# Two projections made in another order by strided matmuls, with contiguous copies, in a recurrence and long-convolution kernel

## The chip, the cores and the metric

The kernel runs on one core of a Trainium2 chip. The metric is the time of one execution on the device in microseconds (us), the median of three runs. Inside the core, five engines run side by side, each with its own queue of instructions in order: PE (TensorE, matrix products), DVE (VectorE), ACT (ScalarE), POOL (GpSimd) and SP (SyncE, which here issues the transfers). PEld stands for the weight loads of PE. On-chip memory is SBUF, and the banks that matmuls write are PSUM.

## What is computed

Two layers, one after the other, on 4 batches of 6272 time steps and 256 channels. First a gated recurrence, then a layer that multiplies two projections of its result with a circular convolution of a third.

```python
sig = 1.0 / (1.0 + np.exp(-f_logit))
f = lower_bound + (1.0 - lower_bound) * sig
for t in range(S):
    h = f[:, t] * h + (1.0 - f[:, t]) * x[:, t]
    y[:, t] = h
...
proj = y @ w_proj                        # 256 -> 3 * 256
x1, x2, x3 = the three thirds of proj
x2_conv = irfft(rfft(x2, axis=1) * rfft(filter_fft, axis=0), n=S, axis=1)
out = (x1 * x2_conv * x3) @ w_out
```

## The kernel before, in words

The state h is held for a whole batch in SBUF (tile HA) as fp16, channels on partitions and time along the free dimension, in two halves `kh` of 128 channels that start at columns HB[0] and HB[1]. The transform of length 6272 = 128 x 49 is split by the prime-factor method: time t is 49 m + r, with m from 0 to 127 and r from 0 to 48 (Q = 49). Between the two halves of h lies a region "A" of the same tile. It holds copies of h that continue a half past its end (the wraps), and later the spectrum.

The work of a batch b goes through these functions:

- `hgrn(b)`: 13 chunks of 512 steps. Two loads per chunk (f_logit and x, on SP), a sigmoid on ACT (L283), a product on POOL (L285), transposes on PE (L294), the gate's affine step from PSUM on ACT (L306) and the scan on DVE (L311), which writes h. After each scan a copy of h into region A (L320, the wraps), which the planner gives to DVE (it appears as L257) or POOL (L262).
- `phase_p(b)`: x2, by matmuls whose weights are columns of h taken at a stride of 49 (L590).
- `phase_f1(b)`: the first transform (L605), evicted by ACT or DVE into region A.
- `mini(b)`: a small transform of the frequencies at index 0 (L620). Its moving operand takes one fp16 of every 128.
- `units(b)`: 16 units. Each loads its part of the filter's spectrum (SP), transforms (L649, moving operand in runs of 64 fp16), multiplies on DVE (L659), copies zero frequencies on POOL (L652) and transforms back (L669); the result is evicted by ACT or DVE.
- `gate(b, u)`, called at the end of unit u: for the chunks in GATES[u], x1 and x3 for 10 values of m, so 490 steps (the last chunk 8, 392 steps), for two blocks `jb` of output channels. Two matmuls for each of x1 and x3 (L340) accumulate over `kh`; two ACT copies (L350) take them from PSUM to the tiles x1s and x3s; one product on POOL (L355) writes z. Each PSUM result is in the order (m, r) of time. The copies put it in the order (r, m) as they write, with steps of 40 bytes in SBUF (32 for the last chunk). There are 104 such matmuls and 52 such copies in a batch.
- `phase_o(b)`: the last transform (L695), the product with z on DVE (L702), the output projection (L712), evictions and the stores (SP).

The order on each engine comes from a planner (class Plan). Every piece of work is entered by `op` with the tokens that it reads and writes and its cost on each engine that may run it. `emit` then places piece after piece: among those whose inputs are placed it takes, for every engine, the one that can start first by these costs, and of equal ones the one with the longest path behind it. Where two engines are given, it chooses by the same costs. So a cost changes the order and the engine, and no instruction. `hgrn(b + 1)` overlaps units and `phase_o(b)`, and its first transposes of a chunk wait for a unit named in AFTER. A gate's matmuls wait for their chunks of h ("hn") and, by the token ("F", u), for the forward transform of their unit. The token "qT" is written by each group of transposes in turn, so that they keep their order.

Of the kernel before, what the change touches and what calls it, by code (L numbers as in the profile page):

```python
# [13 lines left out]
AOP = mybir.AluOpType  # L14
AF = mybir.ActivationFunctionType
# [9 lines left out]
Q = 49  # L25
# [3 lines left out]
NCHK = 13  # L29

AFTER = (2, 5, 7, 10, 12, 15)

GATES = [[u] if u < NCHK else [] for u in range(16)]
XR = 10
NEP = 128
UE = 8
# [2 lines left out]
ZS = 64.0  # L39
# [16 lines left out]
class Plan:  # L56
# [20 lines left out]
    def op(self, cost, fn, r=(), w=(), kb=0.0, table=None, take=0, src=None):  # L77
        preds = set()
        for t in r:
            if t in self.writer:  # L80
                preds.add(self.writer[t])
        for t in w:
            if t in self.writer:
                preds.add(self.writer[t])
            preds.update(self.readers.get(t, ()))
        me = len(self.ops)
        if src is not None:
            preds.add(src)
            self.ops[src]["users"].append(me)
        self.ops.append(dict(cost=cost, fn=fn, preds=preds, kb=kb, table=table, end=None,  # L90
                             eng=None, succ=[], take=take, src=src, users=[], at=None))
        for p in preds:
            self.ops[p]["succ"].append(me)
        for t in r:
            self.readers.setdefault(t, set()).add(me)
        for t in w:
            self.writer[t] = me
            self.readers[t] = set()
        return me
# [89 lines left out]
def kernel(  # L189
# [10 lines left out]
    nc = tc.nc  # L200
# [4 lines left out]
    op = plan.op  # L205
# [12 lines left out]
    W13 = konst.tile([128, 2, 512], F16, name="W13")  # L218
# [5 lines left out]
    HA = konst.tile([128, 2 * S + EW], F16, name="HA")  # L224
    A = HA[:, S:S + EW].rearrange("m (e r k) -> m e r k", r=2, k=64)
    HB = (0, S + EW)
# [5 lines left out]
    x1s = konst.tile([128, 2, CH], F32, name="x1s")  # L232
# [5 lines left out]
    PS = psp.tile([128, 8, 512], F32, name="PS")  # L238

    def E(a, z):  # L240

        return [("E", u) for u in range(a // 1024, (z - 1) // 1024 + 1)]
# [6 lines left out]
    def copy(e, dst, src, scale=None):  # L249
        if e == "ACT":  # L250
            if scale is None:
                nc.scalar.copy(dst, src)  # L252
            else:
                nc.scalar.activation(dst, src, AF.Copy, scale=scale)
        elif e == "DVE":
            if scale is None:
                nc.vector.tensor_copy(dst, src)  # L257
            else:
                nc.vector.tensor_scalar(dst, in0=src, scalar1=scale, scalar2=None,
                                        op0=AOP.mult)  # L260
        else:
            nc.gpsimd.tensor_copy(dst, src)  # L262

    def either(n, runs=1.0):

        return {"ACT": 0.06 + runs * n / 1200.0, "DVE": 0.08 + runs * n / 960.0}

    count = dict(x=0, f=0, s=0, o=0)

# [1 line left out]
    def hgrn(b):  # L271
        for c in range(NCHK):
            t0 = c * CH
            nb = min(CH, S - t0) // 128
            n = nb * 128
            k = count["x"] % NX
            count["x"] += 1
            xt, ft = XT[:, k, 0:nb], FL[:, k, 0:nb]
            for dst, src, t in ((ft, f_logit, ("ft", k)), (xt, x, ("xt", k))):
                op({"SP": 0.5}, lambda e, dst=dst, src=src, t0=t0, n=n: nc.sync.dma_start(  # L280
                    dst, src[b, t0:t0 + n, :].rearrange("(j p) d -> p j d", p=128)),
                   w=[t], kb=n)
            op({"ACT": 0.1 + 0.213 * nb}, lambda e, ft=ft: nc.scalar.activation(  # L283
                ft, ft, AF.Sigmoid, scale=-1.0), r=["sin"], w=[("ft", k)], table="sigmoid")
            op({"POOL": 0.1 + 0.535 * nb}, lambda e, xt=xt, ft=ft: nc.gpsimd.tensor_tensor(  # L285
                xt, xt, ft, op=AOP.mult), r=[("ft", k)], w=[("xt", k)])

            late = [("U", AFTER[min(c, len(AFTER) - 1)])] if b else []
            for kh in range(2):
                cols = slice(kh * 128, kh * 128 + 128)  # L290

                def turn(e, p, src, cols=cols, nb=nb):
                    for j in range(nb):
                        nc.tensor.transpose(PS[:, p, j * 128:(j + 1) * 128], src[:, j, cols],  # L294
                                            iden[:])
                sT = op({"PE": 0.108 * nb}, lambda e, p, f=turn, s=ft: f(e, p, s),
                        r=[("ft", k), "iden"] + late, w=["qT"], take=1)
                uT = op({"PE": 0.108 * nb}, lambda e, p, f=turn, s=xt: f(e, p, s),
                        r=[("xt", k), "iden"], w=["qT"], take=1)
                j = count["f"] % 2  # L300
                count["f"] += 1
                fT = fTs[:, j, 0:n]
                t1 = HB[kh] + t0
                h = HA[:, t1:t1 + n]
                op({"ACT": 0.13 + n / 1200.0}, lambda e, p, fT=fT, n=n, kh=kh:
                   nc.scalar.activation(fT, PS[:, p, 0:n], AF.Identity,  # L306
                                        scale=nomc[:, kh:kh + 1], bias=1.0),
                   r=["om"], w=[("fT", j)], src=sT)
                init = 0.0 if c == 0 else HA[:, t1 - 1:t1]
                op({"DVE": 0.07 + 2.25 * n / 1000.0}, lambda e, p, h=h, fT=fT, n=n, init=init:  # L310
                   nc.vector.tensor_tensor_scan(h, fT, PS[:, p, 0:n], init, op0=AOP.mult,  # L311
                                                op1=AOP.add),
                   r=[("fT", j)] + ([("hn", kh, c - 1)] if c else []), w=[("hn", kh, c)],
                   src=uT)

                a, o = (t0, t0) if kh == 0 else (max(t0, S - E1), EW - S + max(t0, S - E1))
                z = min(t0 + n, E0) if kh == 0 else t0 + n
                if z <= a:
                    continue
                op({"DVE": 0.08 + (z - a) / 3840.0, "POOL": 0.1 + (z - a) / 1000.0},  # L320
                   lambda e, a=a, o=o, z=z, kh=kh: copy(
                       e, HA[:, S + o:S + o + z - a], HA[:, HB[kh] + a:HB[kh] + z]),
                   r=[("hn", kh, c)], w=E(o, o + z - a))


    def gate(b, u):
        z = zt[b % 2]
        for c in GATES[u]:
            m0 = c * XR
            nm = min(XR, 128 - m0)  # L330
            hn = [("hn", kh, i) for kh in range(2) for i in range(max(c - 1, 0), c + 1)]
            t0, n = m0 * Q, nm * Q
            for jb in range(2):
                x13 = []
                for i in range(2):
                    js = slice(i * 256 + jb * 128, i * 256 + jb * 128 + 128)

                    def mm(e, p, js=js, t0=t0, n=n):
                        for kh in range(2):
                            nc.tensor.matmul(PS[:, p, 0:n], W13[:, kh, js],  # L340
                                             HA[:, HB[kh] + t0:HB[kh] + t0 + n],
                                             start=(kh == 0), stop=(kh == 1))
                    x13.append(op({"PE": 2 * n / 2400.0}, mm,
                                  r=hn + ["W13", ("F", u)], w=["qX"], take=1))
                j = count["s"] % 2
                count["s"] += 1
                xs = [t[:, j, 0:n] for t in (x1s, x3s)]
                for i in range(2):
                    op({"ACT": 0.16 + n / 1200.0}, lambda e, p, xs=xs[i], n=n, nm=nm, i=i:
                       nc.scalar.activation(  # L350
                           xs.rearrange("p (r m) -> p m r", m=nm),
                           PS[:, p, 0:n].rearrange("p (m r) -> p m r", r=Q), AF.Copy,
                           scale=1.0 if i else ZS), w=[("x1s", j, i)], src=x13[i])
                op({"POOL": 0.12 + 2.2 * n / 1000}, lambda e, xs=xs, nm=nm,
                   zz=z[:, jb, :, m0:m0 + nm]: nc.gpsimd.tensor_tensor(  # L355
                       zz, xs[0].rearrange("p (r m) -> p r m", m=nm),
                       xs[1].rearrange("p (r m) -> p r m", m=nm), op=AOP.mult),
                   r=[("x1s", j, 0), ("x1s", j, 1)], w=[("z", b % 2, jb, c)])


# [276 lines left out]
    def units(b):  # L637
        for u in range(NU):
# [26 lines left out]
            def inv(e, ib, k=k):  # L665
# [10 lines left out]
                PS[:, ib:ib + 2, 0:392].rearrange("p a (g c) -> p c a g", g=4)),  # L676
               r=[("x2", g) for g in range(13)], w=["Th", ("Th", u)], src=i2)
            gate(b, u)


# [112 lines left out]
```

## Time and profile before

| | us |
|---|---|
| three runs | 624.77, 627.38, 632.55 |
| median | 627.38 |
| the profiled execution | 630.62 |
| its span, first to last instruction | 628.7 |

| engine | busy us | share of the span |
|---|---|---|
| PE | 514.8 | 82% |
| ACT | 489.0 | 78% |
| DVE | 484.3 | 77% |
| PEld | 373.3 | 59% |
| POOL | 300.9 | 48% |

The profile is of one execution. A busy PE is not a PE at its peak: a matmul's row lasts until its result has passed through, and the next one starts meanwhile. The mean granted clock of PE was 0.939 of full speed. A row of a group gives its line, engine, operation, what is written from what, shape and count, then busy time and the mean length of one in ns, and behind the second bar the engine's idle time before such instructions. A row in order of time gives the start, the length from first start to last end, and the number of instructions merged. By the groups, the ACT copies of L350 are the longest part of ACT: 113.0 us for x1s and 113.9 us for x3s.

### The profile page before, as it was taken

Reading aid. Unit: us, or ns where it says so; the run is one execution under the profiler, and the core shown is the slowest. Engines: PE = TensorE matmul, PEld = TensorE weight load, DVE = VectorE, ACT = ScalarE, POOL = GpSimd, SP = SyncE. Lnnn points to the kernel's source line nnn. Section 1 sums busy time; section 2 is a strip of 40 time slices with the busy share of each in tenths; the row PEclk is TensorE's granted clock in tenths of the full one; section 3 lists DMA queues with packets and bytes.
Section 4 is the critical chain, followed back from the end, with each engine's and each line's share of the span. In section 5 each row is a group of like instructions: output and inputs, shape, how many; then the busy total and the mean of one; then the engine's idle time right before and its main releaser. Section 6 shows DMA issues by size and latency. Waiting matters only on the chain.

```text
span 628.7 us, 12525 instructions
## 1 busy us (share of the span) xinstructions
PE 514.8 (82%) x4821; PEld 373.3 (59%) x4821; DVE 484.3 (77%) x490; ACT 489.0 (78%) x578; POOL 300.9 (48%) x312
## 2 busy tenths in 40 slices
PE   0789977888988877888979968889889978888694
PEld 0677756734557767544557757545457768344383
DVE  8977876867888887857968997958789878757562
ACT  4777764879997667989986666989996669799834
POOL 4353452346776444155765443256884530366500
PEclk9877997979999899989999998989999989799988
DMA  9965888123768885033748984036578940234046
GB/s 317 329 231 185 282 283 263 34 84 101 234 193 233 323 302 176 27 104 105 235 145 277 313 304 138 27 103 193 159 241 304 330 157 1 78 103 129 27 168 243
DMA packets 73037, 117.57 MB, mean 187 GB/s; under 512 B 4366, under 2 KB 55634, under 8 KB 72978
## 3 DMA queue, kind: packets, MB, share of 16 engines
q1 hardware_dynamic: 72978, 116.77, 56.4%
q8 instruction: 38, 0.62, 0.4%
q14 instruction: 21, 0.17, 0.1%
HBM read 84.54 MB, written 32.11 MB: 186 GB/s over the span
## 4 chain that ended last, share of the span: by engine, by line
PE 38%; ACT 24%; DMA 13%; DVE 11%; issue 9%; POOL 4%; SPq 0%; ACTq 0%; DVEq 0%; POOLq 0%
ACT x3s L350 8%; PE PS L340 7%; ACT x1s L350 7%; PE PS L294 7%; PE PS L590 6%; DMA H<-HA 4%; ACT X L252 4%; PE PS L712 4%; PE PS L669 4%; DMA FL<-in_f_logit_dram 4%; PE PS L649 3%; DVE HA L311 3%; POOL XT L285 3%; DVE HA L257 3%; DMA XT<-in_x_dram 2%
## 5 line engine op out<-in xcount | busy, mean ns | idle before, releaser
L355 POOL TENSOR_TENSOR z<-x1s,x3s 128x490 f16<-128x490 f32 (+1 forms) x104 | 126.7, 1220 | 142.0 <-ACT x3s L350 136.1
L659 DVE TENSOR_TENSOR PP<-PS,Hu 98x1008 f16<-98x1008 f32 x128 | 147.3, 1201 | 52.9 <-ACT x3s L350 24.0
L285 POOL TENSOR_TENSOR XT<-XT,FL 128x1024 f32<-128x1024 f32 (+1 forms) x52 | 119.2, 2293 | 83.7 <-DMA XT<-in_x_dram 43.0
L311 DVE TENSOR_TENSOR_SCAN HA<-fTs,HA,PS 128x512 f16<-128x512 f32 (+1 forms) x96 | 114.7, 1205 | 26.0 <-PE PS L294 12.8
L350 ACT ACTIVATE x1s<-PS 128x490 f32<-128x490 f32 (+1 forms) x104 | 113.0, 1086 | 4.6 <-PE PS L340 4.3
L340 PE MATMUL PS<-HA,W 128*128 128x490 f16 (+1 forms) x416 | 108.9, 373 | 8.8 <-ACT x1s L350 5.3
L350 ACT ACTIVATE x3s<-PS 128x490 f32<-128x490 f32 (+1 forms) x104 | 113.9, 1095 | 0.1
L252 ACT CAST X<-PS 128x784 f16<-128x784 f32 (+2 forms) x80 | 84.5, 1070 | 22.8 <-PE PS L669 12.1
L306 ACT ACTIVATE fTs<-PS,nomc 128x512 f32<-128x512 f32 (+1 forms) x104 | 68.8, 672 | 39.3 <-PE PS L294 32.7
L294 PE MATMUL PS<-iden,FL 128*128 128x128 f32 x392 | 66.5, 293 | 19.3 <-ACT FL L283 17.1
L294 PE MATMUL PS<-iden,XT 128*128 128x128 f32 x392 | 68.3, 298 | 16.1 <-POOL XT L285 15.0
L702 DVE TENSOR_TENSOR ys<-PS,z 128x1024 fp32r<-128x1024 f32 (+1 forms) x52 | 59.4, 1151 | 18.5 <-PE PS L695 16.5
L669 PEld LDWEIGHTS <-PP 98*128 98x128 f16 x1024 | 54.6, 103 | 28.1 <-POOL PP L652 13.0
L340 PEld LDWEIGHTS <-W 128*128 128x128 f16 x416 | 36.4, 98 | 58.3 <-issue 40.3
L712 PE MATMUL PS<-Wo,ys 128*128 128x256 f32 x392 | 62.5, 304 | 6.5 <-DVE ys L702 5.3
L283 ACT ACTIVATE FL<-FL 128x1024 f32<-128x1024 f32 (+1 forms) x52 | 53.0, 1022 | 17.6 <-DMA FL<-in_f_logit_dram 17.5
L669 PE MATMUL PS<-VA,PP 98*128 98x98 f16 x512 | 57.1, 216 | 11.1 <-POOL PP L652 7.8
L294 PEld LDWEIGHTS PS<-iden,FL 128*128 128x128 f32 x392 | 49.1, 150 | 28.6 <-issue 13.4
L294 PEld LDWEIGHTS PS<-iden,XT 128*128 128x128 f32 x392 | 46.7, 150 | 29.7 <-POOL XT L285 18.8
L649 PE MATMUL PS<-HA,FT 64*128 64x512 f16 x256 | 48.6, 402 | 15.0 <-ACT x3s L350 6.5
L257 DVE CAST X<-PS 128x1024 f16<-128x1024 f32 (+2 forms) x36 | 47.0, 1331 | 17.9 <-PE PS L590 14.3
L712 PEld LDWEIGHTS PS<-Wo,ys 128*128 128x128 f32 x392 | 52.3, 199 | 12.1 <-DVE ys L702 6.8
(90 smaller groups left out, 674.5 us busy)
## 6 DMA issues: line engine op xcount, KB each, us to landing
Hu<-H SPq DMA_DIRECT2D x64, 392.0 KB
FL<-in_f_logit_dram SPq DMA_DIRECT2D x48, 512.0 KB
XT<-in_x_dram SPq DMA_DIRECT2D x48, 512.0 KB
out_dram<-X SPq DMA_DIRECT2D x24, 512.0 KB
out_dram<-osb SPq DMA_DIRECT2D x24, 512.0 KB
HA<-in_moe_filter_fft_dram SPq DMA_DIRECT2D x12, 512.0 KB
H<-HA SPq DMA_DIRECT2D x16, 196.0 KB
H<-HA SPq DMA_DIRECT2D x32, 98.0 KB
```

The costliest lines, as they stand in the source:

```text
L252: nc.scalar.copy(dst, src)
L285: op({"POOL": 0.1 + 0.535 * nb}, lambda e, xt=xt, ft=ft: nc.gpsimd.tensor_tensor(xt, xt, ft, op=AOP.mult), r=[("ft", k)], w=[("xt", k)])
L294: nc.tensor.transpose(PS[:, p, j * 128:(j + 1) * 128], src[:, j, cols], iden[:])
L306: nc.scalar.activation(fT, PS[:, p, 0:n], AF.Identity, scale=nomc[:, kh:kh + 1], bias=1.0),
L311: nc.vector.tensor_tensor_scan(h, fT, PS[:, p, 0:n], init, op0=AOP.mult, op1=AOP.add),
L340: nc.tensor.matmul(PS[:, p, 0:n], W13[:, kh, js], HA[:, HB[kh] + t0:HB[kh] + t0 + n], start=(kh == 0), stop=(kh == 1))
L350: nc.scalar.activation(xs.rearrange("p (r m) -> p m r", m=nm), PS[:, p, 0:n].rearrange("p (m r) -> p m r", r=Q), AF.Copy, scale=1.0 if i e ...
L355: zz=z[:, jb, :, m0:m0 + nm]: nc.gpsimd.tensor_tensor(zz, xs[0].rearrange("p (r m) -> p r m", m=nm), xs[1].rearrange("p (r m) -> p r m", m ...
L649: nc.tensor.matmul(PS[:, xb + e2, :], FT[rows, r, :], A[rows, es, r, :], start=(r == 0), stop=(r == 1))
L659: nc.vector.tensor_tensor(PP[:TB, k, o, :, :, 1:64], px.unsqueeze(1).broadcast_to([TB, 2, UE, 63]), hh[:, :, :, 1:64], op=AOP.mult)
L669: nc.tensor.matmul(PS[:, ib + o, pr * TB:(pr + 1) * TB], PP[:TB, k, o, n, 2 * pr:2 * pr + 2, :], v[:TB], start=(n == 0), stop=(n == 1))
L712: nc.tensor.matmul(po[:, i, :], y[:, kh, i * 128:(i + 1) * 128], Wo[:, kh, :], start=(kh == 0), stop=(kh == 1))
```

## The change

The moving operand of the gate's matmuls is the same stretch of h, now read as (r, m): for each r, ten elements that are 49 fp16 apart. The result stands in PSUM in the order (r, m), one column after another, so both ACT copies read and write without steps. POOL's product takes the same views of x1s and x3s as before. The gates of chunks 0, 1 and 2 belong to unit 0 and depend on the batch's last transposes ("qT") in place of the unit's forward transform; the next ten chunks belong to units 1 to 10. The wraps may run on POOL only. The planner's costs of evictions, of the affine step and of the gate's copies are changed.

```diff
-GATES = [[u] if u < NCHK else [] for u in range(16)]
+GATES = [[0, 1, 2], [3], [4], [5], [6], [7], [8], [9], [10], [11], [12]] + [[]] * 5
...
-        return {"ACT": 0.06 + runs * n / 1200.0, "DVE": 0.08 + runs * n / 960.0}
+        return {"ACT": 0.15 + runs * n / 1200.0, "DVE": 0.15 + runs * n / 960.0}
...
-                op({"ACT": 0.13 + n / 1200.0}, lambda e, p, fT=fT, n=n, kh=kh:
+                op({"ACT": 0.24 + n / 1200.0}, lambda e, p, fT=fT, n=n, kh=kh:
...
-                op({"DVE": 0.08 + (z - a) / 3840.0, "POOL": 0.1 + (z - a) / 1000.0},
+                op({"POOL": 0.1 + (z - a) / 1000.0},
...
-                            nc.tensor.matmul(PS[:, p, 0:n], W13[:, kh, js],
-                                             HA[:, HB[kh] + t0:HB[kh] + t0 + n],
-                                             start=(kh == 0), stop=(kh == 1))
+                            nc.tensor.matmul(PS[:, p, 0:n].rearrange("j (r m) -> j r m", r=Q), W13[:, kh, js],
+                                             HA[:, HB[kh] + t0:HB[kh] + t0 + n]
+                                             .rearrange("k (m r) -> k r m", r=Q), start=(kh == 0), stop=(kh == 1))
...
-                                  r=hn + ["W13", ("F", u)], w=["qX"], take=1))
+                                  r=hn + ["W13", ("F", u) if u else "qT"], w=["qX"], take=1))
...
-                    op({"ACT": 0.16 + n / 1200.0}, lambda e, p, xs=xs[i], n=n, nm=nm, i=i:
+                    op({"ACT": 0.15 + n / 1200.0}, lambda e, p, xs=xs[i], n=n, i=i:
                        nc.scalar.activation(
-                           xs.rearrange("p (r m) -> p m r", m=nm),
-                           PS[:, p, 0:n].rearrange("p (m r) -> p m r", r=Q), AF.Copy,
-                           scale=1.0 if i else ZS), w=[("x1s", j, i)], src=x13[i])
+                           xs, PS[:, p, 0:n], AF.Copy, scale=1.0 if i else ZS),
+                       w=[("x1s", j, i)], src=x13[i])
```

More of the change, by code (lines that the diff above doesn't have):

```diff
@@ L348, in gate @@
                 for i in range(2):
-                    op({"ACT": 0.16 + n / 1200.0}, lambda e, p, xs=xs[i], n=n, nm=nm, i=i:
+                    op({"ACT": 0.15 + n / 1200.0}, lambda e, p, xs=xs[i], n=n, i=i:
                        nc.scalar.activation(
-                           xs.rearrange("p (r m) -> p m r", m=nm),
-                           PS[:, p, 0:n].rearrange("p (m r) -> p m r", r=Q), AF.Copy,
-                           scale=1.0 if i else ZS), w=[("x1s", j, i)], src=x13[i])
-                op({"POOL": 0.12 + 2.2 * n / 1000}, lambda e, xs=xs, nm=nm,
+                           xs, PS[:, p, 0:n], AF.Copy, scale=1.0 if i else ZS),
+                       w=[("x1s", j, i)], src=x13[i])
+                op({"POOL": 0.12 + 2.2 * n / 1000}, lambda e, xs=xs,
                    zz=z[:, jb, :, m0:m0 + nm]: nc.gpsimd.tensor_tensor(
-                       zz, xs[0].rearrange("p (r m) -> p r m", m=nm),
-                       xs[1].rearrange("p (r m) -> p r m", m=nm), op=AOP.mult),
+                       zz, xs[0].rearrange("p (r m) -> p r m", r=Q),
+                       xs[1].rearrange("p (r m) -> p r m", r=Q), op=AOP.mult),
                    r=[("x1s", j, 0), ("x1s", j, 1)], w=[("z", b % 2, jb, c)])
```

## The prediction, made before the change was run

> **What bounds the kernel now.** I read the chain of waits first, then busy time by stage, then the groups with shapes kept apart, then the order of time inside a stage. The chain names the gate's copies and matmuls as its largest lines:
>
> ```profile
> PE 38%; ACT 24%; DMA 13%; DVE 11%; issue 9%; POOL 4%; SPq 0%; ACTq 0%; DVEq 0%; POOLq 0%
> ```
>
> I cut the span where the trace starts the first matmul of line 590 (P), 649 (units) and 695 (output) of each batch. Columns: stretch, its length, busy time of PE, PEld, DVE, ACT, POOL, clock, DMA share, GB/s.
>
> ```profile
> 124.30:194.00 69.70, 61.47 (x544) 35.06 (x543) 53.07 (x50) 64.83 (x80) 46.74 (x52) 0.95 0.52 156
> 194.00:239.00 45.00, 35.10 (x374) 30.22 (x374) 38.85 (x38) 27.43 (x36) 21.68 (x18) 0.96 0.87 292
> 239.00:260.40 21.40, 19.22 (x226) 18.17 (x227) 16.56 (x14) 19.19 (x20) 5.10 (x3) 1.00 0.26 87
> 260.40:329.50 69.10, 58.01 (x488) 32.30 (x487) 52.07 (x49) 62.82 (x76) 41.59 (x47) 0.96 0.47 140
> 534.00:596.00 62.00, 50.92 (x448) 25.67 (x449) 40.58 (x37) 56.96 (x68) 36.05 (x42) 0.94 0.29 85
> ```
>
> The units stage (four times, 62.0 to 69.7 us; the third is 68.7) is bound by ACT, busy 92% of it. All gates run there. Output with the next batch's scan (45.0 us) is DVE and DMA; the P/F1 stage (21.4 to 23.0 us) is PE, then evictions. PE's busy time holds each matmul's latency, so I take PE's load from the pace of starts:
>
> ```profile
> 260.43 0.61 PE L649 MATMUL PS<-HA,FT 64*128 64x512 f16 x4
> 260.96 1.00 PE L340 MATMUL PS<-HA,W 128*128 128x490 f16 x4
> 261.90 0.59 PE L620 MATMUL PS<-HA,FT 64*128 64x128 f16 x4
> ```
>
> Four gate matmuls take 1.00 us and one lasts 0.37, so one starts every (1.00 - 0.37) / 3 = 0.21 us. Line 649 works as pairs on two halves of the rows: (0.61 - 0.40) = 0.21 us a pair. Likewise line 669 starts every 0.043 us, a transpose (294) every 0.11. PE's load in the first units stage is then 104 x 0.21 + 32 x 0.21 + 256 x 0.043 + 84 x 0.11 = 48.8 us of 69.7: it has 20 us to spare, ACT has 5.
>
> **The price that decides** is that of a moving operand read with a stride of 49 fp16 (98 bytes). Three groups bear on it:
>
> ```profile
> L620 PE MATMUL PS<-HA,FT 64*128 64x128 f16 x16 | 2.4, 382 | 0.0
> L605 PE MATMUL PS<-D,X 128*128 128x128 f16 x512 | 32.0, 219 | 7.6 <-DVE X L257 3.6 <-ACT X L252 3.3
> L590 PEld LDWEIGHTS <-HA 128*128 128x128 f16 x392 | 44.5, 144 | 10.5 <-DVE HA L311 8.8
> L340 PEld LDWEIGHTS <-W 128*128 128x128 f16 x416 | 36.4, 98 | 58.3 <-issue 40.3
> ```
>
> Line 620 is the only matmul here whose moving operand jumps at every column (128 fp16, 256 bytes). At 128 columns it lasts 382 ns, where line 605, contiguous, lasts 219. In the order of time its second pair starts 0.59 - 0.39 = 0.20 us after the first, so 128 columns pass in 0.196 us: 1.53 ns a column. By durations it is (382 - 219) / 128 more than the 0.42 of line 340: 1.69; for a pair's first matmul (373 ns) 1.62. I take 1.57: **490 columns in 0.77 us instead of 0.21.** The lower bound is the weight load: line 590 loads the same h with the same stride of 49 in 144 ns, against 98 contiguous, 0.36 ns a column more, so 0.77 ns, 0.375 us a matmul. The lowest is no charge at all, 0.21, since no row shows 98 bytes on the moving side. The upper comes from ACT's row, below: 1.65 ns, 0.81 us.
>
> [...]
>
> **The change part by part, for the likeliest case.**
>
> ACT's copies. In the order of time they start 0.87 us apart (275.22, 276.09), with writes 40 bytes apart. Contiguous evictions of 1024 elements (line 252 to HA, three in 2.88 us, the last 1.03) start 0.92 apart; line 254's forms (1024 elements 1021 ns, 256 elements 375) give (1021 - 375) / 768 = 0.84 ns an element, so 0.06 is fixed. The strided copy then takes (0.87 - 0.06) / 490 = 1.65 ns an element, and contiguous it will take 490 x 0.84 + 0.06 = 0.47 us: 208 x 0.40 = 83 us less on ACT, 20 us in each units stage. That leaves ACT at 45 of 69 there, and DVE (53, less at most 4.6 for line 257) next; the gain is real only as far as PE allows.
>
> PE in units. In the changed program's own order, 24 of a batch's 104 gate matmuls come before the units: 8 before phase P, 8 between P and F1, 8 inside F1. So 80 remain: 80 x 0.77 = 61.6, and 6.7 (649) + 11.0 (669) + 9.2 (294; 6.6 in the second batch, 0 in the last) give 88.5, 85.9, 88.5, 79.3 us. PE's queue is in order, so every forward and inverse transform stands behind gate matmuls four times as long; DVE's products and ACT's copies wait for them. For waits I add 3%, an estimate (phase P of the second batch, PE alone, took 11.5 us where its starts need 98 x 0.11 = 10.8). Stages 91.2, 88.5, 91.2, 81.7 against 69.7, 69.1, 68.7, 62.0: **+83 us**.
>
> P/F1. Each group of 8 is 6.2 us. The first meets 1 to 2.3 us in which PE waits for the last scan; the second the 1.6 to 2 us before F1; the third F1's 8.2 us, of which PE's starts need 7.1. So (6.2 - 2) + (6.2 - 1.7) + (6.2 - 1.1) = 13.8 us, four times: **+55 us**. The 12 copies (5.6 us of ACT) and 6 products (7 us of POOL, otherwise 5 of 21) fit beside the longer PE.
>
> Wraps. All 50 DVE wraps go to POOL, 50 to 100 at 0.61 us: 8 us a batch, POOL from 21.7 to about 30 of 45. DVE loses the 5 to 8 us that line 257 takes in an output stage, where it is busy 86%. On the other side POOL's in-order queue puts the next chunk's product (line 285, 2.4 us) behind wraps that wait for a scan; transposes and then scans wait for that product. Its 8 wraps already wait 11.6 us for scans in 194 to 239. Between -3 and +3 us in each of three stages; I take 0, since both ends rest on DMA at 0.87. Behind the last scan, up to three wraps (1.5 us) stand before phase P: hidden by the first 6.2 us of gates.
>
> The planner's constants move some evictions between ACT and DVE (8 F1 copies to DVE, 4 output copies): below 5 us a batch, on engines with slack once PE bounds. The dependency on "qT" holds the next batch's first transposes back until chunks 0 to 2 are gated, long past. GpSimd's product has the same views as before. Transfers are the same in number and size, all on SP's queue, where the new plan may issue a load some places earlier or later behind the same waits; the span's gates load none.
>
> Sum: 628.7 + 83 + 55 = 767 span, 769 with the 1.9 us outside it. The profiled execution (630.62) is 3.2 above the median of three (627.38): **765 us.** Each 0.1 us of pace is worth 416 x 0.1 x 1.03 = 43 us, so 0.70 to 0.81 give 735 to 782, and waits of 8% instead of 3% some 17 more: this case's own range is 735 to 799.
>
> **The rivals.**
>
> *The weights' price* (0.375 us), the case that ends not slower: PE in units 80 x 0.375 + 26.9 = 57 us, with 8% of waits, as ACT shows now, 61.5, and 58.6, 61.5, 51.5: -36 us. P/F1: 3 groups of 3.0, less 4.8 hidden: +17. So 608 to 610. For it: same tensor, same stride. [...] It decides from about 0.42 us a matmul, where gain and loss meet; below that the change isn't slower.
>
> *Free stride* (0.21): DVE bounds the units at some 53 of 69, the last at an estimated 48; -62 us, P/F1 up to +8 (24 x 0.21 less what the gaps hide), so about 573. For it: line 649 jumps 256 bytes after every 64 columns without loss. Against it: line 620.
>
> *POOL or the plan*: stride cheap, but POOL's wraps delay the scans by more than DVE gains, 3 us a stage, and the constants misplace copies: 640. Little speaks for it while POOL is below half busy.
>
> *The copies don't get faster*: if the 0.87 isn't from the stride, ACT stays at 65 beside PE's 88: still 765.
>
> **How the numbers follow.** 0.66 for the high price (the nearest moving operand[...]), 0.19 for the weights' price, 0.12 for a free stride, 0.03 for POOL or the plan. A measurement of this kernel can tell about 2%, 615 to 640, from no change. Faster: 0.12 and under half of 0.19: 0.20. Same: 0.10. Slower: 0.70. The range 605 to 800 leaves out the free stride (0.12), the low end of the weights' price (0.04) and the top of the likeliest case (0.04).
>
> **What would show it.** Line 340's matmuls starting 0.77 us apart; units stages of 80 to 90 us with ACT near 45 and PE the longest of the chain; P/F1 of 35 us; copies 0.47 us apart; output stages unchanged within 3 us. Starts below 0.42 us would make the forecast wrong, and then DVE or ACT should end the waits in the units.

## The result, and the profile after

The changed kernel takes 963.51 us (median of 4, 957.61 to 965.82) against 629.96 us in the same rounds: 1.532 times the time, 95% interval 1.518 to 1.547. Slower was forecast, at 765 us; the measured time lies far above the range of 605 to 800. Where the forecast saw one price, the trace shows two. From the gate's product on, the changed kernel's line numbers are one lower: L648 is the old L649, L668 the old L669.

The page of the changed kernel, its engines, the granted clock in 40 slices and the chain of waits:

```profile
PE 880.4 (92%) x4821; PEld 440.2 (46%) x4821; DVE 468.4 (49%) x450; ACT 425.0 (44%) x568; POOL 326.2 (34%) x362
...
PEclk9898785556589886555579786566569886555558
...
PE 80%; DMA 9%; POOL 4%; ACT 2%; issue 2%; DVE 2%; SPq 1%; POOLq 0%; ACTq 0%; DVEq 0%
PE PS L340 42%; PE PS L668 9%; PE PS L294 8%; PE PS L648 6%; PE PS L589 5%; DMA XT<-in_x_dram 4%; PE PS L604 4%; PE PS L711 3%; POOL XT L285 3%; PE PS L694 2%; DMA out_dram<-osb 1%; DMA H<-HA 1%; DMA out_dram<-X 1%; DMA wcol<-in_lower_bound_dram 1%; DVE HA L311 1%
```

PE is the bound, with 80% of the chain, and its clock falls to half in long stretches that weren't there before (mean 0.705 against 0.939). The groups of the same page, with length in ns and idle time:

```profile
L340 PE MATMUL PS<-HA,W 128*128 128x490 f16 (+1 forms) x416 | 417.5, 1142 | 0.0
...
L350 ACT ACTIVATE x1s<-PS 128x490 f32<-128x490 f32 (+1 forms) x104 | 59.7, 574 | 165.4 <-PE PS L340 134.4
...
L668 PE MATMUL PS<-VA,PP 98*128 98x98 f16 x512 | 88.2, 277 | 9.2 <-POOL PP L651 9.2
...
L668 PE MATMUL PS<-VB,PP 98*128 98x98 f16 x512 | 88.7, 278 | 0.0
```

The same groups in the page of before:

```profile
L350 ACT ACTIVATE x1s<-PS 128x490 f32<-128x490 f32 (+1 forms) x104 | 113.0, 1086 | 4.6 <-PE PS L340 4.3
L340 PE MATMUL PS<-HA,W 128*128 128x490 f16 (+1 forms) x416 | 108.9, 373 | 8.8 <-ACT x1s L350 5.3
...
L669 PE MATMUL PS<-VA,PP 98*128 98x98 f16 x512 | 57.1, 216 | 11.1 <-POOL PP L652 7.8
```

A gate matmul lasts 1142 ns on average where it lasted 373. The copies did become contiguous and shorter (574 ns, before 1086), and now wait for PE: ACT, which was to be relieved, now stands idle. L668, which the change doesn't touch, went from 216 to 277 ns.

By stage (units, output, P/F1, units of batches 1 and 2, then the last units; columns as in the prediction's table):

```profile
141.40:271.00 129.60, 127.30 (x484) 45.59 (x483) 53.35 (x49) 43.73 (x67) 40.33 (x46) 0.61 0.27 83
271.00:321.00 50.00, 44.23 (x424) 33.74 (x424) 34.43 (x32) 30.17 (x39) 27.40 (x30) 0.91 0.89 303
321.00:357.20 36.20, 35.99 (x243) 21.65 (x241) 18.91 (x15) 21.55 (x24) 10.90 (x7) 0.88 0.00 1
357.20:486.80 129.60, 127.30 (x468) 45.25 (x468) 48.29 (x44) 43.32 (x67) 36.09 (x44) 0.53 0.24 74
803.50:921.50 118.00, 114.56 (x408) 32.78 (x408) 41.33 (x38) 35.63 (x56) 28.31 (x36) 0.52 0.15 45
```

Counted from first matmul to first matmul, units take 118 to 130 us instead of 61 to 69, at a clock of 0.52 to 0.61. P/F1 takes 36 to 39 us (forecast 35). From the first output matmul to the first of phase P it is 50 to 59 us instead of 45 to 48, and that stretch now ends with eight gate matmuls (7.7 us). The order of time inside a units stage shows the two prices side by side:

```profile
371.53 4.02 PE L340 MATMUL PS<-HA,W 128*128 128x490 f16 x4
...
376.79 1.04 PE L648 MATMUL PS<-HA,FT 64*128 64x512 f16 x4
```

Four gate matmuls of 1.13 to 1.15 us take 4.02 together, so they start 0.96 us apart, 4.6 times as far as before (0.21). The forward transform, unchanged, takes 1.04 us instead of 0.61.

### The profile page after: what moved, and what is told of

Its sections match the earlier page's. It is cut to its first block, busy times and chain, and to the rows that moved or that the text cites. A ratio compares the mean times of both kernels' runs of the same rounds, so it can differ in the third digit from the quotient of the medians.

```text
span 955.8 us, 12552 instructions
## 1 busy us (share of the span) xinstructions
PE 880.4 (92%) x4821; PEld 440.2 (46%) x4821; DVE 468.4 (49%) x450; ACT 425.0 (44%) x568; POOL 326.2 (34%) x362
## 4 chain that ended last, share of the span: by engine, by line
PE 80%; DMA 9%; POOL 4%; ACT 2%; issue 2%; DVE 2%; SPq 1%; POOLq 0%; ACTq 0%; DVEq 0%
PE PS L340 42%; PE PS L668 9%; PE PS L294 8%; PE PS L648 6%; PE PS L589 5%; DMA XT<-in_x_dram 4%; PE PS L604 4%; PE PS L711 3%; POOL XT L285 3%; PE PS L694 2%; DMA out_dram<-osb 1%; DMA H<-HA 1%; DMA out_dram<-X 1%; DMA wcol<-in_lower_bound_dram 1%; DVE HA L311 1%
## 5 line engine op out<-in xcount | busy, mean ns | idle before, releaser
L340 PE MATMUL PS<-HA,W 128*128 128x490 f16 (+1 forms) x416 | 417.5, 1142 | 0.0
L340 PEld LDWEIGHTS <-W 128*128 128x128 f16 x416 | 46.1, 125 | 207.9 <-issue 206.7
L350 ACT ACTIVATE x1s<-PS 128x490 f32<-128x490 f32 (+1 forms) x104 | 59.7, 574 | 165.4 <-PE PS L340 134.4
L668 PEld LDWEIGHTS <-PP 98*128 98x128 f16 x1024 | 87.2, 141 | 96.3 <-issue 66.3
L350 ACT ACTIVATE x3s<-PS 128x490 f32<-128x490 f32 (+1 forms) x104 | 59.7, 574 | 153.3 <-PE PS L340 152.7
L668 PE MATMUL PS<-VA,PP 98*128 98x98 f16 x512 | 88.2, 277 | 9.2 <-POOL PP L651 9.2
L294 PE MATMUL PS<-iden,FL 128*128 128x128 f32 x392 | 76.9, 328 | 17.0 <-ACT FL L283 17.0
L668 PE MATMUL PS<-VB,PP 98*128 98x98 f16 x512 | 88.7, 278 | 0.0
L262 POOL COPY HA<-HA 128x512 f16<-128x512 f16 (+3 forms) x100 | 58.9, 596 | 61.4 <-DVE HA L311 59.2
L257 DVE CAST HA<-PS 128x1024 f16<-128x1024 f32 x36 | 43.1, 1222 | 60.3 <-PE PS L604 56.9
```

Source lines behind the costliest of these rows:

```text
L340: nc.tensor.matmul(PS[:, p, 0:n].rearrange("j (r m) -> j r m", r=Q), W13[:, kh, js], HA[:, HB[kh] + t0:HB[kh] + t0 + n] .rearrange("k (m r ...
L350: nc.scalar.activation(xs, PS[:, p, 0:n], AF.Copy, scale=1.0 if i else ZS),
L668: nc.tensor.matmul(PS[:, ib + o, pr * TB:(pr + 1) * TB], PP[:TB, k, o, n, 2 * pr:2 * pr + 2, :], v[:TB], start=(n == 0), stop=(n == 1))
```

## The experiments

Theory S: the strided read makes the whole loss, by its own price and by a halved clock. Rival P: the new places of gates and wraps, or the plan, share in it. Two kernels cut the change in half.

**The changed kernel with the strided read undone** (its matmuls and copies as before, all else as changed).

```diff
-  nc.tensor.matmul(PS[:, p, 0:n].rearrange("j (r m) -> j r m", r=Q), W13[:, kh, js], HA[...].rearrange("k (m r) -> k r m", r=Q), ...)
+  nc.tensor.matmul(PS[:, p, 0:n], W13[:, kh, js], HA[:, HB[kh] + t0:HB[kh] + t0 + n], ...)
...
-  xs, PS[:, p, 0:n], AF.Copy, ...
+  xs.rearrange("p (r m) -> p m r", m=nm), PS[:, p, 0:n].rearrange("p (m r) -> p m r", r=Q), AF.Copy, ...
```

> The changed kernel with the gate's matmuls reading h contiguously and the two copies writing with steps again; gates of unit 0, wraps on POOL and the planner's costs as changed. Theory S (the strided read alone makes the loss): 615 to 650 us, gate matmuls 0.21 us apart, clock near 0.94. Rival P (the new places of the gates, POOL's wraps and the costs share in the loss): over 680 us.

Measured 623.06 us, 0.988 of before (0.983 to 0.992). That is theory S's case. The rest of the change is a small gain, of 1.2%.

**The kernel before with the strided read and contiguous copies alone** (the reverse of that diff, on the kernel before).

> The kernel before with the strided read and the contiguous copies alone; gates, wraps and costs as before. Theory S: 930 to 1000 us, gate matmuls 0.97 us apart, clock near 0.7. Rival P: below 880 us, since the early gates and the wraps are left out.

Measured 962.71 us, 1.526 (1.507 to 1.545): the full loss, at a clock of 0.692. Rival P falls.

**What a stepped operand costs, by itself.** A kernel that only streams matmuls, copies and products. Two of its streams, the flat step of 98 bytes (49 fp16) and the gate's order; `warm` issues 40 contiguous matmuls, and `ap` gives the operand's dimensions as (step, count):

```diff
+        for _ in range(16):
+            nc.tensor.matmul(PS[:, 0, 0:490], Wt[:], T[:, 0:23962:49], start=True, stop=True)
+        warm()
...
+        for _ in range(40):
+            nc.tensor.matmul(PS[:, 0, 0:490].rearrange("j (r m) -> j r m", r=49), Wt[:], ap(T, [[1, 49], [49, 10]]), start=True, stop=True)
+        warm()
```

> No part of the computation: only streams of one matmul of 490 columns, each stream with another pattern of its moving operand and with dense contiguous matmuls between, then the gate's copies and products in other orders; the output is zeros in 512 rows and otherwise not written. Theory L [...]: steps of 16, 32, 98 and 256 bytes all near 1.5 to 2.0 ns a column, and the flat step of 98 bytes as slow as the ten-by-49 order (0.97 us). Rival B [...]: a flat step of 98 bytes near 0.7 ns a column (0.35 us), multiples of 128 bytes slower, and the jump back after each ten columns makes up the rest. Theory C [...]: clock 0.5 inside the strided streams, 1.0 in the dense ones; rival: clock 1.0 in both. Copy that reads PSUM with steps and writes contiguously: 0.5 us if only the write's steps cost, 0.87 or more if the read's do too.

Its groups on PE. The steps are: L74 the gate's order (runs of ten at 98 bytes, 49 runs), L56 96 bytes flat, L59 98 flat, L50 32, L47 16, L71 256, L44 8, L104 a contiguous read with a PSUM write in steps of 40 bytes, L41 4 bytes:

```profile
L74 PE MATMUL PS<-T,Wt 128*128 128x490 f16 x40 | 38.8, 1151 | 0.0
L56 PE MATMUL PS<-T,Wt 128*128 128x490 f16 x16 | 19.8, 1420 | 0.0
L59 PE MATMUL PS<-T,Wt 128*128 128x490 f16 x16 | 17.0, 1238 | 0.0
...
L50 PE MATMUL PS<-T,Wt 128*128 128x490 f16 x16 | 14.2, 1059 | 0.0
...
L47 PE MATMUL PS<-T,Wt 128*128 128x490 f16 x16 | 13.9, 1040 | 0.0
...
L71 PE MATMUL PS<-T,Wt 128*128 128x490 f16 x16 | 13.3, 996 | 0.0
...
L44 PE MATMUL PS<-T,Wt 128*128 128x490 f16 x16 | 7.1, 610 | 0.0
L104 PE MATMUL PS<-T,Wt 128*128 128x490 f16 x16 | 6.7, 613 | 0.0
...
L41 PE MATMUL PS<-T,Wt 128*128 128x490 f16 x16 | 3.6, 378 | 0.0
```

The pace is (busy - length of one) / (count - 1): L74 (38.8 - 1.15) / 39 = 0.97 us, as in the kernel; L59 1.05; L56 1.23; L50 0.88; L47 0.86; L71 0.82; L44 0.43; L41 0.22, against 0.21 contiguous. In ns a column: 0.44 at 4 bytes, 0.88 at 8, 1.75 at 16, 1.80 at 32, 1.67 at 256, 2.15 at 98, 2.50 at 96. So theory L's 1.5 to 2.0 ns holds at 16, 32 and 256 bytes and fails at 96 and 98: beyond 16 bytes the price still hangs on the step. And it begins below 16: steps of 8 already run at half the pace (0.43 against 0.21 us). Rival B's 0.7 ns a column, about the price of the weight load, is refuted: the flat step of 98 bytes is no cheaper than the ten-by-49 order, but dearer (1.05 against 0.97 us).

The clock, in stretches of the 8-byte stream, then the gate's order (PE busy, PEld, DVE, ACT, POOL, clock):

```profile
102.10:108.60 6.50, 6.50 (x17) 1.71 (x16) 0.00 (x0) 0.00 (x0) 0.00 (x0) 1.00 0.00 0
...
340.40:378.00 37.60, 37.60 (x40) 4.98 (x39) 0.00 (x0) 0.00 (x0) 0.00 (x0) 0.56 0.00 0
```

Theory C's half clock is there in the gate's order, and not at 8 bytes. PE is busy without a gap in both, but at 0.97 us a matmul the clock falls to half (1.00 in the stream's first 4.3 us, 0.50 from then on), and at 0.43 it stays at 1.00. So the busy time of the rows doesn't tell the clock. That the low clock came with the slow stream was measured; by what mechanism was not shown. What half the clock costs shows in the contiguous matmuls right behind the gate's stream, first while the clock is still low, then when it is back (L36; PE busy, PEld, clock):

```profile
379.10:382.20 3.10, 3.10 (x8) 1.09 (x8) 0.50 0.00 0
382.80:385.90 3.10, 3.10 (x17) 1.47 (x15) 1.00 0.00 0
```

They start 0.41 us apart, then 0.21. The strided matmuls themselves keep their pace (median of starts 0.97 us at half clock and at full): whatever stands between them pays. The changed kernel's own trace agrees: its gate matmuls start 0.966 us apart at either clock, the inverse transform's matmuls start 0.043 us apart at full clock and 0.081 at half, those of F1 0.056 and 0.107.

The same kernel's copies: L109 writes SBUF in steps of 40 bytes, L107 has no steps, L111 reads PSUM in steps of 196 bytes and writes without:

```profile
L109 ACT ACTIVATE X<-PS 128x490 f32<-128x490 f32 x12 | 12.4, 1035 | 0.4
L107 ACT ACTIVATE X<-PS 128x490 f32<-128x490 f32 x12 | 7.0, 579 | 584.8 <-PE PS L104 584.5
L111 ACT ACTIVATE X<-PS 128x490 f32<-128x490 f32 x12 | 7.0, 579 | 0.4
```

This stepped read of PSUM by ACT costs nothing (579 ns both ways), the stepped write of SBUF nearly doubles the copy (1035 ns). PE's own write of PSUM is not free of steps: L104 starts a matmul every 0.41 us against 0.21, at a clock of 1.00.

**The order made by POOL's product.** The kernel before with contiguous matmuls and copies, z written in steps:

```diff
-  xs.rearrange("p (r m) -> p m r", m=nm), PS[:, p, 0:n].rearrange("p (m r) -> p m r", r=Q), AF.Copy, ...
+  xs, PS[:, p, 0:n], AF.Copy, ...
...
-  zz, xs[0].rearrange("p (r m) -> p r m", m=nm), xs[1].rearrange("p (r m) -> p r m", m=nm), op=AOP.mult
+  zz.rearrange("p r m -> p m r"), xs[0].rearrange("p (m r) -> p m r", r=Q), xs[1].rearrange("p (m r) -> p m r", r=Q), op=AOP.mult
```

> The kernel before with contiguous matmuls and contiguous copies; POOL's product reads both without steps and writes z with steps of 256 bytes. If the copies' price (0.87 against 0.47 us) bounded the units and POOL's write costs no more than its arithmetic (1.2 us): 565 to 600 us. If POOL pays for the steps (2 us a product): 600 to 640 us, with the units waiting for POOL.

Measured 659.75 us, 1.046 (1.034 to 1.058), worse than both guesses. Its first two units stages:

```profile
127.30:196.80 69.50, 56.67 (x504) 32.39 (x503) 56.19 (x49) 44.49 (x76) 63.96 (x47) 0.98 0.49 148
271.10:342.10 71.00, 56.91 (x490) 31.43 (x491) 57.73 (x49) 44.27 (x76) 63.93 (x46) 0.95 0.42 131
```

ACT fell to 44 us, but POOL is now at 64. A product takes about 2.0 us instead of 1.22, an estimate: in the last units stage POOL's 42 instructions, 26 of them products, take 57.1 us instead of 36.1. ACT's copies now wait for POOL: the bound only moved.

**The copies read PSUM with steps.** One edit to the kernel before:

```diff
-  xs.rearrange("p (r m) -> p m r", m=nm), PS[:, p, 0:n].rearrange("p (m r) -> p m r", r=Q), AF.Copy,
+  xs.rearrange("p (r m) -> p r m", m=nm), PS[:, p, 0:n].rearrange("p (m r) -> p r m", r=Q), AF.Copy,
```

> The kernel before with one edit: the two copies read PSUM in the order (r, m), with steps of 196 bytes, and write SBUF contiguously; matmuls contiguous. The ladder showed that such a copy lasts as long as a contiguous one (579 ns). Theory A (the copies' writes bound the units, 20 us of ACT in each): 570 to 600 us, copies 0.47 us apart, units stages of 53 to 60 us. Rival D (another engine stands just behind ACT): 605 to 630 us.

Measured 584.27 us, 0.932 (0.923 to 0.941). Two of its units stages:

```profile
127.00:182.10 55.10, 52.40 (x504) 31.11 (x503) 51.61 (x49) 43.15 (x76) 44.28 (x50) 1.00 0.60 180
253.00:309.40 56.40, 52.26 (x490) 29.93 (x491) 50.59 (x49) 43.65 (x76) 40.17 (x47) 0.97 0.56 166
```

ACT gives back about 20 us in each of them, they shrink by 12 to 13 (counted from first matmul to first matmul, from 67.4 and 69.4), and DVE is busy 90 to 94% of them. This is about what a free stride would have brought; its rival put it at 573.

**The same in the changed kernel** (early gates, wraps on POOL and new costs kept, matmuls contiguous).

> The changed kernel (early gates, wraps on POOL, its costs) with contiguous matmuls and copies that read PSUM with steps. Theory A with gains that add (1.2% from the places and wraps): 560 to 595 us and below the kernel with the copies' edit alone. Rival D: within 1% of that kernel, since ACT no longer bounds the units and early gates then relieve nothing.

Measured 580.02 us, 0.919 (0.902 to 0.936), the lowest median. Its interval overlaps that of the copies' edit alone, so the two aren't told apart, as rival D had it.

**Two dials on the price.** The changed kernel with `[o, Q], [step, n // Q]` as the operand's two dimensions, step 4 or 32 elements; o (9 or 4 for 490 columns) keeps the 49 runs inside the same stretch of h.

> The changed kernel with another pattern of the moving operand, ten columns 8 bytes apart and 49 such runs, all inside the same 490 columns of h: x1 and x3 are then made of the wrong time steps, in number and shape the same. The ladder has 432 ns a matmul at 8 bytes, at full clock. If the loss is the price of the read and the halved clock that comes with it: 590 to 640 us, clock 0.9 or more, about the break-even of 0.42 us that the forecast named. If the strided form costs by itself (place of the gates, PE's queue): over 680 us.

> The same with columns 64 bytes apart (again the wrong time steps): the ladder has 820 ns a matmul and half the clock. If price and clock make the loss: 0.145 us less for each of 416 matmuls than in the changed kernel, all on PE's path, so 890 to 910 us with the clock still near 0.7. If it is the price alone, with the clock recovering: near 800 us.

Measured 669.5 us, 1.068 (1.047 to 1.089), and 901.67 us, 1.438 (1.409 to 1.467). The first lies in neither of its ranges, the second in that of price and clock. Groups on PE of the 8-byte dial, then of the 64-byte dial (L344 are the gate's matmuls, L671 the inverse transform):

```profile
L344 PE MATMUL PS<-HA,W 128*128 128x490 f16 x384 | 197.8, 649 | 0.0
...
L671 PE MATMUL PS<-VB,PP 98*128 98x98 f16 x512 | 56.8, 216 | 0.0
```

```profile
L344 PE MATMUL PS<-HA,W 128*128 128x490 f16 x384 | 335.0, 1005 | 0.0
L671 PE MATMUL PS<-VB,PP 98*128 98x98 f16 x512 | 86.0, 273 | 0.0
```

The matmuls start 0.47 and 0.83 us apart (median of the trace; the ladder's flat stream at 8 bytes had 0.43), the clock is 0.946 and 0.723. Between the two dials 416 x 0.36 = 150 us of pace lie, but 232 us of time: some 80 us are left over. The inverse transform, which neither dial touches, lasts 273 ns in the second and 216 in the first, so much of this goes to the clock.

**The three other edits, each alone on the kernel before**: wraps on POOL; the gates' new places and "qT"; the planner's costs.

> The kernel before with the wraps on POOL only. The three other edits of the change together gave 0.988 of the time. Theory W (DVE's relief in the output stages carries it): 0.985 to 0.993. Rival (POOL's queue holds the scans back): 1.00 to 1.015.

> The kernel before with the gates of chunks 0 to 2 moved ahead of the units and the next ten to units 1 to 10; strided writes by the copies stay. Theory G (24 of 104 copies leave the stage that ACT bounds): units stages shorter by 7 to 10 us each, P/F1 longer by 4 to 6, so 0.98 to 0.99 in all. Rival: P/F1 takes all of it back, 1.00.

> The kernel before with the planner's changed costs of evictions, affine step and copies alone: 0.995 to 1.01, since order and engine of a few evictions change and no instruction does.

Measured 1.005 (1.002 to 1.008), 0.985 (0.979 to 0.992), 1.012 (1.004 to 1.020). The early gates gain what theory G had, with units 6 to 9 us shorter and P/F1 about 4 longer. The wraps cost a little (0.5%), so the rival's sign was right, not W's. The costs alone lose slightly more than expected, and the three together (0.988) aren't the product of the three (1.002). The planner makes another order for each of these kernels; which difference in it matters was not followed up.

**Stepped PSUM reads with the early gates.**

> The kernel before with the copies that read PSUM with steps and with the early gates; wraps and costs as before. Theory A with gains that add (0.932 and 0.985): 0.915 to 0.925. Rival (the early gates relieve ACT, which then no longer bounds the units): 0.93 to 0.94, no better than the copies' edit alone.

Measured 588.48 us, 0.934 (0.929 to 0.939): the rival's case. With ACT relieved, moving copies out of the units brings nothing measurable.

## Why the prediction was wrong

**The mechanism was right**: PE takes over the units from ACT, copies shorten (574 ns; forecast 0.47 us apart, measured so in the kernels where PE lets them follow one another), and the strided read is the cause. The size was wrong: the profiled span grew by 955.8 - 628.7 = 327 us, and 138 were forecast. The step that failed is the sum for PE in the units, "80 x 0.77 = 61.6, and 6.7 (649) + 11.0 (669) + 9.2 (294 ...)". Its price was too low, and so were its other three terms, above all because they took PE's clock to stay as it was.

**The price of a matmul: 0.97 us, not 0.77.** The step "I take 1.57 ns a column" read the price from line 620, at 256 bytes. The ladder has 1.67 ns there and 1.97 in the gate's order at 98 bytes. 384 x (0.967 - 0.207) + 32 x (0.900 - 0.165), with the trace's paces of both forms, is 315 us on PE; the forecast's 416 x 0.56 was 233. So 82 us. The upper bound (ACT's 1.65 ns) was no bound: every step of 16 bytes or more that the ladder tried costs more, 1.67 to 2.50 ns.

**The other matmuls, and the clock, which is not in the sum at all.** For transforms and transposes the forecast counted 26.9, 24.3, 26.9 and 17.7 us in the four units stages, 96 us together, from the pace of starts before. PE's busy time in these stages is shown here for the changed kernel, then for the 8-byte dial, which differs from it in the pattern of the operand alone and has a clock of 0.95 in them:

```profile
sum 507.00, PE 496.67 PEld 169.21 DVE 196.41 ACT 166.34 POOL 145.08; mean PE 124.17 PEld 42.30 DVE 49.10 ACT 41.58 POOL 36.27
```

```profile
sum 278.40, PE 267.52 PEld 117.09 DVE 192.72 ACT 161.67 POOL 140.29; mean PE 66.88 PEld 29.27 DVE 48.18 ACT 40.42 POOL 35.07
```

The gate matmuls at their pace (72 of 490 columns and 8 of 392 in each stage) are 307 and 147 us of this. For everything else 189.4 us are left in the changed kernel and 120.2 in the dial. So 69 us came with the lower clock (0.52 to 0.61), and 24 us were missing even at 0.95. Of these 24, some 8 fall on the dial's own short stretches at half clock (an estimate: its transforms spend 17 us in them) and 2 on line 620, which the sum leaves out; the rest was not taken apart.

**The waits were right in the units.** PE stands idle for 507.0 - 496.7 = 10.3 us there; the 3% of the forecast were 10.4.

82 + 69 + 24 = 175 us, of the 327 - 138 = 189 that the forecast missed. The other 14 us lie mostly outside the units and were not taken apart. A slip in the forecast's cuts is small beside this: two of its units stages end 2 us behind the first output matmul (191.7 and 467.5 us in the trace, not 194.0 and 469.5).

**The rivals.** The weights' price is refuted for the moving side, though the tensor and the stride are the same. Its turning point, 0.42 us, was too high: at 0.47 us the dial's span is already 41 us longer. If each 0.1 us is worth 416 x 0.1 = 42 us, it lies near 0.37, an estimate. "Free stride" had the right picture of what the faster copies are worth: 584 measured where the copies read PSUM with steps, 580 with the rest of the change beside it, 573 forecast. POOL's wraps cost 0.5%, inside the -3 to +3 us a stage.

**The range.** Its top rested on one price with an upper bound from another engine's writes. No case in it let PE's own clock answer to the change, although the profile has that column.

## What to carry to other kernels

An order that has to change somewhere should change on the side that was seen not to pay for steps: here ACT's read of PSUM (579 ns with and without), not PE's read of SBUF (0.97 us against 0.21), nor ACT's write to SBUF (1035 ns against 579) or POOL's (2.37 us against 1.22). Price an access pattern with the very step and operand that will run, in a kernel of its own: the same stride in the weight load (0.375 us a matmul) and another stride in the moving operand (0.77) were wrong by factors of 2.6 and 1.3 against the measured 0.97. When a change makes the columns of one kind of matmul come this slowly, count every other matmul near it at the lower clock too: here the mean clock was 0.65 over a stream at 0.82 us for 490 columns and 0.56 at 0.97, and stayed at 1.00 at 0.43.

## What the runs showed of the hardware, unexpected

- A moving operand of fp16 streams at nearly full pace with steps of 4 bytes (0.22 us for 490 columns), at half with 8 (0.43), at a quarter with 16 (0.86), and slower still at 96 and 98 (1.23 and 1.05), while 64, 128 and 256 bytes all give 0.82. What makes 96 bytes the dearest wasn't tried.
- The pace of a matmul in the gate's order doesn't change with the granted clock (0.97 us at half and at full), but the stream brings the clock to 0.50 although PE is busy for all of its 37.6 us. Contiguous matmuls behind it start 0.41 us apart until the clock is back, then 0.21.
- A copy of 490 fp32 from PSUM with steps of 196 bytes takes as long as a contiguous one (579 ns); with a write to SBUF in steps of 40 bytes it takes 1035.
- POOL's product takes 1.22 us with a write in runs of ten fp16, 2.37 with elements 256 bytes apart, 1.90 with reads in steps of 196 bytes.
